# One core, local attention into two expert layers: finished rows transposed through a bank of their own and last in the step; the second batch's scale in later steps

## Chip, cores, metric

The kernel runs on one core of one Trainium2 chip, as one launch. The metric is the device time of the execution in microseconds (us). The median of three executions of the kernel before is given with the lowest and the highest; the trace is of one profiled execution.

## What is computed

The reference is an attention with a local window and 32 global tokens, followed by a gated layer and a routed layer with eight experts. For each of 4 batches and 8 heads (512 local and 32 global tokens, 64 wide):

```
s_ll = scale * q_l @ k_l.T, masked to |i - j| <= 32
s_l  = concat(scale * q_l @ k_g.T, s_ll)
out_l = softmax(s_l) @ concat(v_g, v_l)
out_g = softmax(scale * q_g @ concat(k_g, k_l).T) @ concat(v_g, v_l)
x = rows of concat(out_g, out_l)                  # 2304 tokens, 512 wide
x = (silu(x @ w_gate) * (x @ w_val)) @ w_out      # 1536 inner columns
# then routing by x @ w_gate2 to 8 experts of 288 tokens each, relu(x @ w1) @ w2
```

## The kernel before, in words

All of it is one program on one core; TensorE, VectorE, ACT and GpSimd work side by side, SP issues the transfers. The local attention is cut into 32 units (batch, half of the sequence, pair of heads), each with two windows of 128 queries. Units 0 to 15 (batches 0 and 1) are done by `front()` before anything else; the other 16 and the global tokens are worked in between the blocks of the first expert layer later. Four units with the same half make two tiles of 128 finished rows of 512, 256 tokens together; `x0_t` transposes a tile, so that it can be the moving operand of the gated layer, and splits it into a high half in fp16 (`xth`, by ACT) and a low half (`xtl`, the difference, by VectorE). The first three 256-token blocks are worked through together by `first_blocks()` (`gates` makes the two inner products, `out` the product with `w_out`), the rest by `moe_block()`; then come routing and the eight experts.

`front()` is a pipeline by hand, one window a step, steps 0 to 37. In step s it works on four windows:
- window s: its scores, four matmuls into bank S or X1 (`t` is the unit's tile);
- window s - 1: VectorE takes mask and maximum (`sm`, two rows), ACT the exponential (`pb`);
- window s - 2: TensorE transposes `pb` into a bank PTa or PTb (`pt_()` gives them in turn), ACT makes the high half `pth`, VectorE the low half `ptl`;
- window s - 3: `st_c` multiplies with the values, twelve small matmuls into bank PV; in odd steps `st_d` divides the unit by its sums (three rows of VectorE: `rs`, its reciprocal, `x`).

In between, in the order written, stand: one call in step s of the generator `V1 = v_all(1, True)`; `v_mul` and `v_cut` (GpSimd scales and splits a unit's values, ACT makes their high half `vh`); a call of `x0_t` if a finished tile is waiting in `later` (two come from `st_d` in each of steps 11, 19, 27 and 35, one is taken there and one in the step after); a piece of `conv()`, by `step_conv`, which turns the 64-bit weights into fp16 and fp32 pieces (mostly one row of VectorE, at times one of ACT); and, at the end, `ptl`.

`v_all(1, True)` finds the scale of batch 1's values in seven calls: load of half 0 into the buffer `gkr`, its sums of magnitudes on ACT (`v_sums`, two rows of ACT with their accumulator reads), load of half 1 into the same buffer, its sums, then three calls of `v_scale`: a maximum over the partitions with `bound` (a transpose of one column, a maximum on VectorE, a product with ones, in two pt_() tiles), and the power of two on VectorE. `v_mul` of unit 8 needs it in step 17.

From step 4 on, `ve`, `sc`, `te` and `gp` are wrapped by `InOrder` (line 50), which makes each instruction of the front follow the one before it on its engine; the trace therefore puts all of them down to L50. Instructions of other functions, `first_blocks()` above all, are not tied and are put in between by the compiler's own schedule. SP isn't wrapped.

PSUM has eight banks here: S, PV, PTa, PTb, X0, X1, and two of G. `front()` uses S, X1, PV, PTa and PTb. `XTAGS` gives the output banks of the first three blocks: X0 and X1, S and PV, PTa and PTb.

Of the kernel before, what the change touches and what calls it, by code (L numbers as in the profile page):

```python
# [33 lines left out]
def body(ctx, tc, units, gk, gv, wts, w2g, w1, w2, cst, cst2, out):  # L34
# [40 lines left out]
    def mark(ins):  # L75

        TURN[:] = [ins]
# [10 lines left out]
    def psb(tag):  # L88

        return ps.tile([128, 512], F32, name=tag, tag=tag, bufs=2 if tag == "G" else 1)  # L90

    def pt_():

        pts[0] ^= 1
        return psb("PT" + "ab"[pts[0]]).rearrange("p (c q) -> p c q", c=4)
# [10 lines left out]
    def load_unit(u):  # L106

        while UQ and UQ[0] <= u + (4 if UQ[0] < 4 * NA else 2):
            v = UQ.pop(0)
            if v < 4 * NA and v % 8 < len(PLACES):  # L110
                t = PLACES[v % 8]
            else:
                t = ld.tile([128, UW], F32, name="unit", bufs=UB)
            sy.dma_start(t, units[v])
            UT[v] = t
# [3 lines left out]
    def gk_tile():  # L119
        return ld.tile([128, 1280], F32, name="gkr", bufs=1)  # L120
# [58 lines left out]

    def bound(src):  # L180

        pt = pt_()
        te.transpose(pt[:1, 0, :], src, ident)
        m = wk.tile([1, 1], F32, name="pm", bufs=2)
        ve.tensor_reduce(m, pt[:1, 0, :], axis=AX.X, op=OP.max)
        yield
        pt = pt_()
        te.matmul(pt[:, 0, :1], one[:1], m, start=True, stop=True)
        yield pt[:, 0, :1]

# [79 lines left out]
    def v_sums(b, g):  # L270

        if g == 0:
            VM[b] = wk.tile([128, 4], F32, name="vm2", bufs=2)
        r = GVT.pop((b, g)).rearrange("p c w -> p (c w)")
        for i in range(2):
            sc.activation(junk, r[:, 640 * i:640 * i + 640], AF.Abs, accum_out=VM[b][:, 2 * g + i:2 * g + i + 1])

    def v_scale(b):
        m = wk.tile([128, 1], F32, name="vm", bufs=2)
        ve.tensor_reduce(m, VM.pop(b), axis=AX.X, op=OP.add)  # L280
        ve.tensor_scalar(m, m, 2.0 ** -96, None, op0=OP.max)
        iv = big.tile([128, 1], F32, name=f"iv{b}")
        parts = bound(m)
        next(parts)
        yield
        p = next(parts)
        yield
        VS[b] = pow2(p, 1, iv)
        IVB[b] = iv

    def v_all(b, own):

        for g in range(2):
            load_gv(b, g, own)
            yield
            v_sums(b, g)
            yield
        if own:
            yield from v_scale(b)
            yield  # L300
# [11 lines left out]
    X0 = {}  # L312
# [76 lines left out]
    def st_c(u, w):  # L389
        ph, pl = PTH.pop((u, w))  # L390
        vh, vl = UV[u]
        if w == 0:
            PVB[u] = psb("PV")[:, :260].rearrange("p (w h d) -> p w h d", w=2, h=2)
        pv = PVB[u]
        for h in range(2):
            n = 0
            for c in range(2):
                for a, v, m in ((ph, vh, 65), (ph, vl, 64), (pl, vh, 65)):
                    te.matmul(pv[:, w, h, :m], a[:112, 2 * h + c, :], v[:, 4 * w + 2 * c + h],  # L399
                              start=(n == 0), stop=(n == 5))  # L400
                    n += 1
        if w == 1 and u >= 4 * NA:
            st_d(u)

    def st_d(u):
        pv = PVB[u]
        hp = u % 4
        r = wk.tile([128, 2, 2], F32, name="rs")
        ve.tensor_scalar(r, pv[:, :, :, 64], P15 * 1e-9, None, op0=OP.add)
        ve.reciprocal(r, r)  # L410
        if hp == 0:
            X0[u // 4] = wk.tile([128, 2, DM], F32, name="x0", bufs=1)
        x0 = X0[u // 4]
        ve.tensor_tensor(x0[:, :, 128 * hp:128 * hp + 128].rearrange("p w (h d) -> p w h d", h=2),
                         pv[:, :, :, :64],
                         r[:, :, :, None].to_broadcast([128, 2, 2, 64]), op=OP.mult)
        del PVB[u], UT[u], UV[u]
        KQ.pop(u, None)

    def x0_t(k, src, t, n):  # L420
        if t == 0:
            if k == 2:
                XT[k] = [ld.tile([128, 5, 256], F16, name=n, bufs=1)[:, :4] for n in ("vch", "vcl")]
            elif k == 3:
                p = gk_tile().bitcast(F16)
                XT[k] = [p[:, o:o + 1024].rearrange("p (d t) -> p d t", d=4) for o in (0, 1024)]
            else:
                XT[k] = [wk.tile([128, 4, 256], F16, name=n) for n in ("xth", "xtl")]
        h, l = XT[k]
        pt = pt_()  # L430
        for d in range(4):
            te.transpose(pt[:, d, :], src[:, 128 * d:128 * d + 128], ident)
        s = slice(128 * t, 128 * t + 128)
        sc.activation(h[:, :, s], pt, AF.Copy)  # L434
        ve.tensor_tensor(l[:, :, s], pt, h[:, :, s], op=OP.subtract)  # L435
# [197 lines left out]
    def front():  # L633


        n = 8 * NA
        SS = {}
        nonlocal ve, sc, te, gp
        engines = ve, sc, te, gp
        later = []  # L640
        V1 = v_all(1, True)
        for s in range(n + 6):
            if s == 4:
                ve, sc, te, gp = map(InOrder, engines)
            at = lambda d: divmod(s - d, 2)
            if 2 <= s < n + 2:
                u, w = at(2)
                pt = pt_()
                pb = PB.pop((u, w))
                for h in range(2):  # L650
                    for c in range(2):
                        te.transpose(pt[:112, 2 * h + c, :], pb[:, h, 112 * c:112 * c + 112], ident)
                ph = wk.tile([128, 4, 128], F16, name="pth")
                pl = wk.tile([128, 4, 128], F16, name="ptl")
                sc.activation(ph[:112], pt[:112], AF.Copy, scale=P15)
            if 4 <= s and s % 2 and s - 5 < n:
                u = (s - 5) // 2
                if u >= 0:
                    st_d(u)
                    if u % 4 == 3:  # L660
                        x0 = X0.pop(u // 4)
                        later.extend((u // 4, x0[:, t], t, 256) for t in range(2))
            if 1 <= s < n + 1:
                u, w = at(1)
                S = SS.pop((u, w))
                sm = wk.tile([128, 2, WIN], F32, name="sm", tag="sm")
                mx = wk.tile([128, 2], F32, name="mx")
                for h in range(2):
                    mark(ve.tensor_tensor_reduce(sm[:, h], S[:, h, :WIN], mask[:, 2 * ((u // 4) % 2) + w], -0.125, BIG,
                                                 OP.add, OP.min, mx[:, h:h + 1]))  # L670
                pb = wk.tile([128, 2, WIN], F32, name="pb")
                for h in range(2):
                    sc.activation(pb[:, h], sm[:, h], AF.Exp, bias=mx[:, h:h + 1], scale=-1.0)
                PB[u, w] = pb
            if s < n:
                u, w = at(0)
                t = UT[u]
                S = psb("X1" if w else "S").rearrange("p (h c) -> p h c", h=2)
                for h in range(2):
                    o = UK + 256 * h + 128 * w  # L680
                    te.matmul(S[:, h, :WIN], t[:, o:o + 128], t[:, 128 * w:128 * w + WIN], start=True, stop=True)
                SS[u, w] = S
                if w == 0:
                    load_unit(u)
            if 3 <= s < n + 3:
                st_c(*at(3))
            if s < 2:
                v_sums(0, s)
            if s == 2:
                for _ in v_scale(0):  # L690
                    pass
                v_mul(0)
                v_cut(0)
            if 4 <= s < 12:
                next(V1, None)
            if s % 2 and 3 <= s < n:
                v_mul(s // 2)
            if s % 2 == 0 and 4 <= s <= n:
                v_cut(s // 2 - 1)
            if later and s - 2 < n + 4:  # L700
                x0_t(*later.pop(0))
            if s >= 5:
                step_conv()
            if 2 <= s < n + 2:
                u, w = at(2)
                mark(ve.scalar_tensor_tensor(pl[:112], pt[:112], P15, ph[:112], op0=OP.mult, op1=OP.subtract))
                PTH[u, w] = ph, pl
        while later:
            x0_t(*later.pop(0))
        ve, sc, te, gp = engines  # L710

    def v_mul(u):
        r = UT[u][:112, UK + 512:]
# [611 lines left out]
```

## Time and profile before

| | us |
|---|---|
| median of 3 executions | 960.69 (960.13 to 963.97) |
| profiled execution, its own time | 965.33 |
| its span, first to last instruction | 963.6 |
| TensorE busy | 871.9 (90% of the span) |
| VectorE busy | 611.1 (63%) |
| ACT busy | 453.0 (47%) |
| GpSimd busy | 371.9 (39%) |

The span is what the trace covers; the 1.7 us to the execution's own time lie around it. Starts in the trace are counted from the span's start. PE is TensorE's matmuls, PEld its weight loads, DVE VectorE, POOL GpSimd, SP the transfers' queue. The granted clock is a share of 2.4 GHz. A bracket at a timeline's row gives how long the engine had stood idle before it, and what released it. Names stand for tiles without their buffer numbers; digits at the end of a name are left out.

### The profile page before, as it was taken

Reading aid. Unit: us, or ns where it says so; the run is one execution under the profiler, and the core shown is the slowest. Engines: PE = TensorE matmul, PEld = TensorE weight load, DVE = VectorE, ACT = ScalarE, POOL = GpSimd, SP = SyncE. Lnnn points to the kernel's source line nnn. Section 1 sums busy time; section 2 is a strip of 40 time slices with the busy share of each in tenths; the row PEclk is TensorE's granted clock in tenths of the full one; section 3 lists DMA queues with packets and bytes.
Section 4 is the critical chain, followed back from the end, with each engine's and each line's share of the span. In section 5 each row is a group of like instructions: output and inputs, shape, how many; then the busy total and the mean of one; then the engine's idle time right before and its main releaser. Section 6 shows DMA issues by size and latency. Waiting matters only on the chain.

```text
span 963.6 us, 19509 instructions
## 1 busy us (share of the span) xinstructions
PE 871.9 (90%) x7556; PEld 732.3 (76%) x7556; DVE 611.1 (63%) x1859; ACT 453.0 (47%) x923; POOL 371.9 (39%) x344
## 2 busy tenths in 40 slices
PE   5677699999999999989979989996789989999996
PEld 4566578777788887778758757783488988999996
DVE  3677699999328579597595484268666766763210
ACT  4656454555247465445354333230554364545531
POOL 2444333444212222113111111121666786687841
PEclk8889889999999999989989999997789999999998
DMA  9631243542212233303221020001454455446600
GB/s 373 254 121 45 86 155 132 160 161 66 88 66 93 85 103 108 118 29 109 82 78 56 27 74 1 1 23 43 169 184 142 133 185 188 135 149 215 197 28 26
DMA packets 28497, 108.10 MB, mean 112 GB/s; under 512 B 3572, under 2 KB 3572, under 8 KB 28276
## 3 DMA queue, kind: packets, MB, share of 16 engines
q1 hardware_dynamic: 25332, 97.94, 30.0%
q0 software_dynamic: 3072, 8.92, 2.6%
q8 instruction: 59, 0.97, 0.4%
q14 instruction: 34, 0.28, 0.1%
HBM read 97.92 MB, written 8.91 MB: 111 GB/s over the span
## 4 chain that ended last, share of the span: by engine, by line
PE 68%; DVE 12%; issue 7%; DMA 5%; POOL 4%; ACT 3%; SPq 0%; POOLq 0%; ACTq 0%; DVEq 0%
PE G L564 26%; PE X L588 11%; PE A L1152 7%; PE A L1136 5%; PE rt L961 2%; DMA er<-w 2%; DMA xg<-xs,idx 2%; DVE junk L523 2%; DVE ge L948 1%; POOL wp L50 1%; PE PV L476 1%; PE PV L399 1%; POOL vl L50 1%; PE T L1101 1%; DMA gkr<-gv 1%
## 5 line engine op out<-in xcount | busy, mean ns | idle before, releaser
L564 PEld LDWEIGHTS <-wp 128*128 128x128 f16 x2592 | 231.6, 99 | 80.5 <-issue 52.0
L564 PE MATMUL G<-xth,wp 128*128 128x256 f16 (+1 forms) x1344 | 235.8, 270 | 4.1 <-ACT xth L434 2.5
L578 POOL TENSOR_TENSOR hl<-th,hh 128x256 fp32r<-128x256 f32 (+1 forms) x108 | 85.5, 792 | 348.1 <-ACT hh L576 274.8
L564 PE MATMUL G<-xtl,wp 128*128 128x256 f16 (+1 forms) x672 | 177.5, 270 | 4.3 <-DVE xtl L435 4.3
L1083 POOL TENSOR_TENSOR el<-er,eh 128x1024 fp32r<-128x1024 f32 x62 | 146.3, 2390 | 40.7 <-ACT eh L1080 40.4
L569 ACT ACTIVATE th<-G,ib 128x256 f32<-128x256 f32 (+1 forms) x108 | 49.4, 459 | 107.8 <-PE G L564 97.0
L571 DVE SCALAR_TENSOR_TENSOR th<-th,G 128x256 f32<-128x256 f32 (+1 forms) x108 | 43.4, 402 | 81.9 <-ACT th L569 81.0
L1080 ACT ACTIVATE eh<-er 128x1024 fp32r<-128x1024 f32 x64 | 65.5, 1054 | 49.4 <-DMA er<-w 43.2
L576 ACT ACTIVATE hh<-th 128x256 fp32r<-128x256 f32 (+1 forms) x108 | 43.4, 402 | 75.4 <-DVE th L573 75.1
L1136 PE MATMUL A<-xh,eh 128*128 128x272 f32 x256 | 77.9, 304 | 0.0
L1152 PE MATMUL A<-fh,eh 128*128 128x272 f32 x256 | 76.6, 302 | 0.0
L1136 PE MATMUL A<-xh,el 128*128 128x272 f32 x256 | 75.2, 294 | 0.0
L1136 PE MATMUL A<-xl,eh 128*128 128x272 f32 x256 | 74.9, 293 | 0.0
L1152 PE MATMUL A<-fh,el 128*128 128x272 f32 x256 | 74.4, 292 | 0.0
L1152 PE MATMUL A<-fl,eh 128*128 128x272 f32 x256 | 74.2, 291 | 0.0
L1141 DVE SCALAR_TENSOR_TENSOR fl<-A,fh 128x272 fp32r<-128x272 f32 x64 | 28.0, 439 | 59.2 <-ACT fh L1140 57.4
L523 DVE SCALAR_TENSOR_TENSOR junk<-xr,w2gt 128x512 f16<-128x512 f32 x80 | 59.0, 737 | 4.1 <-ACT xr L500 3.4
L588 PE MATMUL X<-oh,hh 128*128 128x512 f32 x156 | 57.7, 444 | 2.1 <-ACT hh L576 2.1
L588 PE MATMUL X<-oh,hl 128*128 128x512 f32 x156 | 55.7, 428 | 0.0
L573 DVE SCALAR_TENSOR_TENSOR th<-th,ib,G 128x256 f32<-128x256 f32 (+1 forms) x108 | 50.1, 464 | 2.9
L588 PE MATMUL X<-ol,hh 128*128 128x512 f32 x156 | 51.5, 403 | 0.0
L1136 PEld LDWEIGHTS A<-xl,eh 128*128 128x128 f32 x256 | 49.2, 192 | 0.1
(389 smaller groups left out, 2126.7 us busy)
## 6 DMA issues: line engine op xcount, KB each, us to landing
er<-w SPq DMA_DIRECT2D x64, 512.0 KB, 5.2
wr<-wts SPq DMA_DIRECT2D x36, 512.0 KB, 3.6
unit<-units SPq DMA_DIRECT2D x22, 688.0 KB, 4.0
unit<-gv SPq DMA_DIRECT2D x12, 640.0 KB, 3.8
wp<-units SPq DMA_DIRECT2D x10, 688.0 KB, 7.8
gkr<-gk SPq DMA_DIRECT2D x8, 608.0 KB, 4.7
xs<-xr SPq DMA_DIRECT2D x17, 256.0 KB, 2.0
gkr<-gv SPq DMA_DIRECT2D x4, 640.0 KB, 7.3
```

Of the source, the lines that this page charges most:

```text
L523: ve.scalar_tensor_tensor(junk[:, :DM], xr, 1.0, w2gt[:, e], op0=OP.mult, op1=OP.mult, accum_out=L[:, c, e:e + 1])
L564: te.matmul(pg[:, j, :n], wp_[:, f, j, a, o], x[:, d, :n], start=(i == 0), stop=(i == 11))
L569: TH[:] = [sc.activation(th[:, :n], pg[:, 0, :n], AF.Tanh, scale=ib[:, 0, f:f + 1])]
L571: ve.scalar_tensor_tensor(t[:, :n], th[:, :n], 1.0, pg[:, 0, :n], op0=OP.add, op1=OP.mult)
L573: mark(ve.scalar_tensor_tensor(h[:, :n], t[:, :n], ib[:, 1, f:f + 1], pg[:, 1, :n], op0=OP.mult, op1=OP.mult))
L576: sc.activation(hh[:, :n], h[:, :n], AF.Copy)
L578: gp.tensor_tensor(hl[:, :n], h[:, :n], hh[:, :n], op=OP.subtract)
L588: te.matmul(self.px[t], a[:, 128 * t:128 * t + 128], w[:, f, :], start=(f == 0 and i == 0), stop=(f == NF - 1 and i == 2))
L1080: q = sc.activation(h, r, AF.Copy)
L1083: q = (ve if j == 0 and i < 2 else gp).tensor_tensor(l, r, h, op=OP.subtract)
L1136: behind(te.matmul(pa_[:, :CAP], a[:, s], x[:, d], start=(i == 0), stop=(i == 11)))
L1152: behind(te.matmul(py[:, :CAP], a[:, s], x[:, f], start=(i == 0), stop=(i == 23)))
```

## The change

A function `spare()` gives a tile in bank X0 as long as `front()` runs and one by `pt_()` afterwards (`FRONT` is emptied at its end). `bound` and `x0_t` take their banks from it. V1 is called in steps 4, 8, 9, 12, 13, 14 and 15 instead of each step from 4 to 11: the load of half 0 stays in step 4, its sums go from 5 to 8, the load of half 1 from 6 to 9, its sums from 7 to 12, and the three calls of `v_scale` from 8, 9 and 10 to 13, 14 and 15. The call of `x0_t` goes to the end of the step, behind `step_conv` and `ptl`; the condition that is dropped there held in every step.

```
--- before.py
+++ after.py
@@ -88,6 +88,12 @@
     def psb(tag):
 
         return ps.tile([128, 512], F32, name=tag, tag=tag, bufs=2 if tag == "G" else 1)
+
+    FRONT = [True]
+
+    def spare():
+
+        return psb("X0").rearrange("p (c q) -> p c q", c=4) if FRONT else pt_()
 
     def pt_():
 
@@ -179,12 +185,12 @@
 
     def bound(src):
 
-        pt = pt_()
+        pt = spare()
         te.transpose(pt[:1, 0, :], src, ident)
         m = wk.tile([1, 1], F32, name="pm", bufs=2)
         ve.tensor_reduce(m, pt[:1, 0, :], axis=AX.X, op=OP.max)
         yield
-        pt = pt_()
+        pt = spare()
         te.matmul(pt[:, 0, :1], one[:1], m, start=True, stop=True)
         yield pt[:, 0, :1]
 
@@ -427,7 +433,7 @@
             else:
                 XT[k] = [wk.tile([128, 4, 256], F16, name=n) for n in ("xth", "xtl")]
         h, l = XT[k]
-        pt = pt_()
+        pt = spare()
         for d in range(4):
             te.transpose(pt[:, d, :], src[:, 128 * d:128 * d + 128], ident)
         s = slice(128 * t, 128 * t + 128)
@@ -691,23 +697,24 @@
                     pass
                 v_mul(0)
                 v_cut(0)
-            if 4 <= s < 12:
+            if s in (4, 8, 9, 12, 13, 14, 15):
                 next(V1, None)
             if s % 2 and 3 <= s < n:
                 v_mul(s // 2)
             if s % 2 == 0 and 4 <= s <= n:
                 v_cut(s // 2 - 1)
-            if later and s - 2 < n + 4:
-                x0_t(*later.pop(0))
             if s >= 5:
                 step_conv()
             if 2 <= s < n + 2:
                 u, w = at(2)
                 mark(ve.scalar_tensor_tensor(pl[:112], pt[:112], P15, ph[:112], op0=OP.mult, op1=OP.subtract))
                 PTH[u, w] = ph, pl
+            if later:
+                x0_t(*later.pop(0))
         while later:
             x0_t(*later.pop(0))
         ve, sc, te, gp = engines
+        FRONT.clear()
 
     def v_mul(u):
         r = UT[u][:112, UK + 512:]
```

## Rows read from the trace of the kernel before

**Rows 1.** Stretches: us; PE, PEld, DVE, ACT, POOL busy (instructions); granted clock; DMA share; GB/s

```profile
20.00:128.00 108.00, 78.27 (x706) 65.61 (x705) 76.05 (x247) 63.58 (x139) 45.43 (x40) 0.84 0.41 142
128.00:212.80 84.80, 84.80 (x639) 68.11 (x638) 78.22 (x150) 45.80 (x102) 33.53 (x48) 1.00 0.45 150
...
32.50:35.00 2.50, 0.00 (x0) 0.00 (x0) 0.00 (x0) 1.08 (x3) 0.00 (x0) 1.00 0.93 371
37.50:42.50 5.00, 4.63 (x27) 4.20 (x28) 4.44 (x18) 2.01 (x5) 3.10 (x2) 0.50 0.41 123
```

**Rows 2.** Who DVE waited for in 20 to 128 us

```profile
DVE xtl L50 <- ACT xth L50: 10.5, 4, 4.0
...
DVE vcl L50 <- ACT vch L50: 5.6, 2, 3.7
DVE vm L50 <- ACT junk L50: 4.5, 1, 4.5
```

**Rows 3.** Timeline of DVE; start us, us, engine line op, [idle before <-releaser]

```profile
29.85 0.68 DVE L50 SCALAR_TENSOR_TENSOR ptl<-PTa,pth 112x512 f16<-112x512 f32 x1
...
35.61 0.16 DVE L50 TENSOR_REDUCE vm<-vm 128x1 f32<-128x4 f32 x1 [4.47 <-ACT junk L50]
...
43.37 0.69 DVE L50 SCALAR_TENSOR_TENSOR ptl<-PTb,pth 112x512 f16<-112x512 f32 x1 [0.65 <-ACT pth L50]
...
57.53 0.68 DVE L50 SCALAR_TENSOR_TENSOR ptl<-PTa,pth 112x512 f16<-112x512 f32 x1
...
67.81 0.37 DVE L50 CUSTOM_DVE_ANT_0 sm<-X,mask 128x224 f32<-128x224 f32 x1
...
68.43 0.69 DVE L50 SCALAR_TENSOR_TENSOR wp<-wr,wp 128x512 int32<-128x512 int32 x1
69.04 0.69 DVE L50 SCALAR_TENSOR_TENSOR ptl<-PTb,pth 112x512 f16<-112x512 f32 x1
69.64 0.15 DVE L50 TENSOR_SCALAR rs<-PV 128x4 f32<-128x4 f32 x1
...
70.38 0.38 DVE L50 CUSTOM_DVE_ANT_0 sm<-S,mask 128x224 f32<-128x224 f32 x1
...
72.85 0.69 DVE L50 TENSOR_TENSOR xtl<-PTb,xth 128x512 f16<-128x512 f32 x1 [1.77 <-ACT xth L50]
...
74.06 0.68 DVE L50 SCALAR_TENSOR_TENSOR ptl<-PTa,pth 112x512 f16<-112x512 f32 x1
...
81.20 0.69 DVE L50 SCALAR_TENSOR_TENSOR ptl<-PTa,pth 112x512 f16<-112x512 f32 x1
...
94.17 0.67 DVE L50 SCALAR_TENSOR_TENSOR ptl<-PTb,pth 112x512 f16<-112x512 f32 x1
...
108.05 0.68 DVE L50 SCALAR_TENSOR_TENSOR ptl<-PTa,pth 112x512 f16<-112x512 f32 x1
...
119.99 0.68 DVE L50 SCALAR_TENSOR_TENSOR ptl<-PTa,pth 112x512 f16<-112x512 f32 x1
...
130.11 0.69 DVE L50 TENSOR_TENSOR gkr<-PTa,gkr 128x512 f16<-128x512 f32 x1 [0.48 <-ACT gkr L50]
```

**Rows 4.** Timeline of ACT

```profile
33.89 0.74 ACT L50 ACTIVATE junk<-gkr 128x640 f16<-128x640 f32 x1 [4.32 <-DMA gkr<-gv]
...
70.87 0.85 ACT L50 ACTIVATE pb<-sm,mx 128x224 f32<-128x224 f32 x2 [0.24 <-DVE mx L50]
72.22 0.60 ACT L50 ACTIVATE xth<-PTb 128x512 f16<-128x512 f32 x1 [0.51 <-PE PTb L50]
74.18 0.72 ACT L50 ACTIVATE junk<-wp,tiny 128x512 f16<-128x512 f32 x1 [1.36 <-DVE wp L50]
...
76.85 0.62 ACT L50 ACTIVATE vh<-wp 112x512 f16<-112x512 f32 x1
```

**Rows 5.** Timeline of PE

```profile
49.25 0.87 PE L50 MATMUL PTa<-ident,pb 128*112 128x128 f32 x4 [2.44 <-DVE ptl L50]
...
122.50 1.22 PE L588 MATMUL X<-oh,hh 128*128 128x512 f32 x2 [0.68 <-ACT hh L576]
```

More of the change, by code (lines that the diff above doesn't have):

```diff
@@ L90, in psb, with spare @@
         return ps.tile([128, 512], F32, name=tag, tag=tag, bufs=2 if tag == "G" else 1)
+    FRONT = [True]
+    def spare():
+        return psb("X0").rearrange("p (c q) -> p c q", c=4) if FRONT else pt_()
     def pt_():
@@ L180, in bound @@
     def bound(src):
-        pt = pt_()
+        pt = spare()
         te.transpose(pt[:1, 0, :], src, ident)
@@ L186, in bound @@
         yield
-        pt = pt_()
+        pt = spare()
         te.matmul(pt[:, 0, :1], one[:1], m, start=True, stop=True)
@@ L429, in x0_t @@
         h, l = XT[k]
-        pt = pt_()
+        pt = spare()
         for d in range(4):
@@ L693, in front @@
                 v_cut(0)
-            if 4 <= s < 12:
+            if s in (4, 8, 9, 12, 13, 14, 15):
                 next(V1, None)
@@ L699, in front @@
                 v_cut(s // 2 - 1)
-            if later and s - 2 < n + 4:
-                x0_t(*later.pop(0))
             if s >= 5:
@@ L707, in front @@
                 PTH[u, w] = ph, pl
+            if later:
+                x0_t(*later.pop(0))
         while later:
@@ L710, in front @@
         ve, sc, te, gp = engines
+        FRONT.clear()
     def v_mul(u):
```

## The prediction

> **What bounds the kernel now.** I read the page first (TensorE busy nearly throughout, least in the first slices and at a lower clock there), then the stretches, the waits of VectorE, and the timelines of the first attention. The stretches show two regimes [rows 1]. From 128 us on TensorE is busy all the time at 2.4 GHz: what ends earlier before that point ends the program earlier. From 20 to 128 us, where the change lies, TensorE is busy for 78.3 of 108 us at a mean granted clock of 0.84, and VectorE for 76.1: no engine is full, so the steps of `front()` are bound by who waits for whom.
>
> VectorE makes one `ptl` in each step from 2 to 33, so the starts of `ptl` are the clock of the steps: that of step 7 is at 29.85, of step 10 at 43.37, 13 at 57.53, 18 at 69.04, 21 at 81.20, 26 at 94.17, 29 at 108.05, 33 at 119.99 [rows 3]. Steps 14 to 18, without anything special, take (69.04 - 57.53) / 5 = 2.30 us each. Three groups of steps take far more than 3 x 2.30 = 6.9 us:
> - 8 to 10, with the second batch's sums and scale: 13.52 us;
> - 11 to 13, with the first finished rows: 14.16 us;
> - 19 to 21 and 27 to 29, with the second and third pair of row tiles: 12.16 and 13.88 us.
>
> The waits say why [rows 2]. VectorE waited 10.5 + 5.6 = 16.1 us, in six waits, for the high halves (`xth`, `vch`) of `x0_t`, and 4.5 us for the sums of batch 1. TensorE waited for VectorE in turn: the transposes of step 12 stood 2.44 us before `ptl` of step 11 had freed PTa [rows 5], since `x0_t` had taken PTb out of turn.
>
> **The change, part by part.** I take the step's order and durations from the rows and lay the new order out by hand. On VectorE, starts of rows that follow each other give what each takes: `sm` pair 0.62, conversion 0.61, `ptl` 0.60, `st_d` 0.74 (69.64 to 70.38) [rows 3]; an `xtl` row is 0.69, with 0.60 to the next start. On ACT `pb` takes 0.85, an accumulating conversion row 0.72, `vh` 0.62, `xth` 0.60 [rows 4].
>
> *V1 later, steps 8 to 10.* Now the second load for batch 1 waits for the buffer that step 5's sums free, so step 7's sums wait 4.32 us for it [rows 4], VectorE 4.47 for the sums [rows 3], and TensorE stands empty from 32.5 to 35 [rows 1]. Afterwards step 8 sums the first half, step 9 issues the second load, step 12 sums it: some three steps of cover, 7 us or more, while the transfers are at a 0.93 share only until about 35 us. The load's issue moves on SP's queue too: it waits for ACT in step 8, and what stands behind it (unit 10 for step 20, weight words for step 17) is needed some eight steps later, so I cost that at nothing; if the cover failed, ACT would wait in step 12 as it now does in step 7, 4.3 us. In step 8 the sums cost ACT 1.7 us (33.89 until VectorE's `vm` goes at 35.61). Laid out, `ptl` of step 8 goes at 31.5, step 9 at 35.3 (behind sums, `vh`, conversion, `pth` on ACT), step 10 at 37.3: 7.4 us instead of 13.52, **-6.1**. Ends: -4.5 (only VectorE's wait goes) and 6.9 - 13.52 = -6.6.
>
> *Bank and order, steps 19 to 21.* Nothing changes until `sm` of step 18 ends at 71.0. The conversion and `ptl` of step 19 then go at once, to 72.2. The finished rows' transposes are where they were, so `xth` could start at 72.22, but the conversion's ACT row now stands ahead: `xth` about 72.5, `xtl` 73.1 to 73.7. Step 20's transposes find PTb free and run at 72.2, no longer behind `ptl`. But `sm` of step 19 now stands behind `xtl`: 73.7 to 74.3, conversion and `ptl` to 74.9 at the latest; on ACT `pb` starts at 74.05, then `vh`, a conversion row, and `xth` only at 76.1; `xtl` 76.65 to 77.25; then `st_d`, `sm`, conversion: `ptl` of step 21 at 79.25 instead of 81.20, **-2.0**. Three steps then take 10.2 us. Ends: 0 (the wait only changes its place) and 6.9 + 2 x 0.60 - 12.16 = -4.1 (all of it hidden).
>
> A rule of the Trainium skill speaks against the bank: by Perfetto Trace Analysis, Optimizing Tensor Performance (Matmuls), independent groups should rotate through banks, so that emptying one overlaps filling the next, and here every spare tile sits in the one bank X0. By it the second tile would wait for the first's `xtl`. In the layout that costs nothing: X0 is free at 73.7 and the second tile's transposes come up at 73.9, behind `st_c`.
>
> *Steps 27 to 29.* The same 10.2 us against 13.88, **-3.7**; ends 0 and -5.8.
>
> *Steps 11 to 13.* The same 10.2, and now with the sums of step 12 on ACT (1.7) and the scale's way VectorE, TensorE, VectorE in step 13 (some 0.9): 12.8 against 14.16, **-1.4**; ends 0 and -3.3. The scale's end in steps 14 and 15 adds **+0.5**, ends 0 and 1.
>
> *The hand-over.* The fourth pair of tiles (steps 35, 36) isn't needed until block 3, so its place costs nothing by itself. But it now uses X0, and X0 is the first bank into which the first blocks write, at 122.50 [rows 5]; the last `x0_t` has its bank read at 130.11 + 0.69 = 130.80 [rows 3]. TensorE's queue is in order: if the first output waited for it, it would lose up to 8.3 us; nothing, if VectorE ends the tiles first. I take **+2.2**: what is pushed into the full stretch is the six outputs of one block, 3.7 us at the 1.22 us per two of this row, somewhat over half of it at the full clock.
>
> Sum: -6.1 - 2.0 - 3.7 - 1.4 + 0.5 + 2.2 = -10.5 us. The profiled execution took 965.33 us (span 963.6), 4.64 over the median shown, 960.69; the forecast is 954.8 for such an execution, so **950.2** for the median. All ends together: 20 us gained to 5 lost.
>
> **The rivals.**
> - *TensorE gets warmer (0.15).* After the empty stretch the granted clock is 0.50 from 37.5 to 42.5 [rows 1], that is 1.2 GHz. The mean of 0.84 over 108 us says that about a third of them, 35 us, ran at that level. If half of that went and a quarter of its time were on the path, some 4.5 us more are gained: 945.7. The Trainium skill's TensorE: Matmul & The Clock Gate, HAM oscillation, says the same of idle waits between bursts: they bring the half clock back; the empty 2.5 us with 0.50 after them agree. For it: the waits named go. Against: the ones left may still suffice.
> - *The hand-over costs all of its 8.3 us (0.12).* Then -12.7 + 8.3 = -4.4: 956.3, no change to speak of. For it: TensorE's queue is in order, and VectorE gets to the last tile 10 us after the last `ptl` [rows 3]. Against: the output matmuls may be queued behind other work.
> - *The wait only moves, from bank to ACT (0.05 even, 0.08 worse).* `xth` is last on ACT, `xtl` last on VectorE, and the next `sm`, then `pb`, stand behind it. If the three pairs gain nothing, -6.1 + 0.5 + 2.2 = -3.4: 957.3. If each of the six steps loses an ACT `pb` and `vh` on top, about 1.5 us, that is 9 us: 966.3, slower. It decides from 3.4 / 6 = 0.57 us per step: VectorE's mean wait before `xtl` would have to rise from 16.1 / 6 = 2.7 to over 3.3 us. Against: the order by hand gives it 0.4 and 1.7.
> That the change doesn't do what it says is unlikely: on VectorE, ACT, TensorE and GpSimd `front()` runs in written order from step 4.
>
> **How the numbers follow.** The forecast has 0.60, the rivals the rest. A measurement can tell about 0.5%, 4.8 us. Faster by more: 0.60 + 0.15 = 0.75; within: 0.12 + 0.05 = 0.17; slower: 0.08. The range goes from 944 (the warm rival and half of what the upper ends add to it) to 958 (past the two cases without change).
>
> **What would show it.** Right: `ptl` of step 10 near 37 us, no ACT wait on the `gkr` load, `ptl` of 19 and 20 no longer behind `xtl`; `ptl` of step 33 near 107; from there the same tail with the full stretch at 117 or 118. Wrong: a wait of over 2 us before `xtl` in most of the six steps; an X output matmul that waits for the last `xtl`; or a full stretch that starts earlier and yet ends as late.

## The result, and the profile after

The changed kernel takes 949.41 us (median of 4 executions, 943.45 to 952.47) against 961.79 (960.13 to 963.97) for the kernel before in the same comparison: ratio 0.9861, 95% interval 0.9821 to 0.9901, 1.4% faster. Its profiled execution took 952.47 us, span 950.7, against 965.33 and 963.6: 12.9 us less. TensorE's busy time is the same, 871.8 us to 871.9. Lines moved by six: L564, L576 and L588 of the kernel before are L570, L582 and L594 here.

The stretches of the changed kernel, with the columns of [rows 1]:

```profile
20.00:118.00 98.00, 79.48 (x723) 65.27 (x723) 78.18 (x253) 66.03 (x145) 49.28 (x45) 0.84 0.48 166
118.00:201.40 83.40, 83.40 (x624) 66.79 (x623) 76.55 (x144) 43.69 (x97) 32.41 (x44) 1.00 0.45 142
32.50:35.00 2.50, 2.21 (x22) 1.56 (x21) 2.43 (x10) 2.47 (x6) 0.50 (x1) 1.00 0.90 359
37.50:42.50 5.00, 5.00 (x44) 4.53 (x43) 3.61 (x13) 3.90 (x9) 3.52 (x3) 0.66 0.92 302
```

The full stretch starts 10 us earlier. Ahead of it TensorE does the same work (79.5 us, before 78.3) in 98 us where it took 108, so its idle time there fell from 29.7 to 18.5 us. The stretch that was empty is full (2.21 of 2.50 us). The granted clock of the stretch from 37.5 to 42.5 us rose from 0.50 to 0.66, but its mean over the front is 0.84, as before.

The waits of VectorE in 20 to 118 us (us in total, times, longest) answer to [rows 2]:

```profile
DVE xtl L50 <- ACT xth L50: 5.3, 4, 2.0
...
DVE vcl L50 <- ACT vch L50: 1.5, 2, 1.0
```

16.1 us before the low halves became 6.8, and the 4.5 us for the sums of batch 1 are gone from the list. VectorE's timeline, to be read beside [rows 3]:

```profile
31.49 0.68 DVE L50 SCALAR_TENSOR_TENSOR ptl<-PTa,pth 112x512 f16<-112x512 f32 x1
...
38.66 0.69 DVE L50 SCALAR_TENSOR_TENSOR ptl<-PTb,pth 112x512 f16<-112x512 f32 x1 [0.49 <-ACT pth L50]
...
48.00 0.69 DVE L50 TENSOR_TENSOR xtl<-X,xth 128x512 f16<-128x512 f32 x1 [2.05 <-ACT xth L50]
...
51.56 0.67 DVE L50 SCALAR_TENSOR_TENSOR ptl<-PTa,pth 112x512 f16<-112x512 f32 x1
...
65.82 0.68 DVE L50 SCALAR_TENSOR_TENSOR ptl<-PTa,pth 112x512 f16<-112x512 f32 x1
67.27 0.69 DVE L50 TENSOR_TENSOR xtl<-X,xth 128x512 f16<-128x512 f32 x1 [0.76 <-ACT xth L50]
...
70.86 0.69 DVE L50 TENSOR_TENSOR xtl<-X,xth 128x512 f16<-128x512 f32 x1 [1.68 <-ACT xth L50]
...
73.49 0.68 DVE L50 SCALAR_TENSOR_TENSOR ptl<-PTa,pth 112x512 f16<-112x512 f32 x1
...
107.03 0.68 DVE L50 SCALAR_TENSOR_TENSOR ptl<-PTa,pth 112x512 f16<-112x512 f32 x1
...
119.62 0.69 DVE L50 TENSOR_TENSOR gkr<-X,gkr 128x512 f16<-128x512 f32 x1 [0.82 <-ACT gkr L50]
```

These are `ptl` of steps 7 (31.49), 10, 13 (51.56), 19 (65.82), 21 (73.49) and 33. `ptl` of step 19 stands 1.45 us ahead of the low half of its finished rows; before, it stood behind it (`xtl` 72.85, `ptl` 74.06 [rows 3]). ACT, beside [rows 4]:

```profile
33.54 0.72 ACT L50 ACTIVATE junk<-gkr 128x640 f16<-128x640 f32 x1
...
45.29 0.72 ACT L50 ACTIVATE junk<-gkr 128x640 f16<-128x640 f32 x1
...
46.87 0.61 ACT L50 ACTIVATE vh<-unit 112x512 f16<-112x512 f32 x1
47.39 0.58 ACT L50 ACTIVATE xth<-X 128x512 f16<-128x512 f32 x1
```

The first sums (33.54) and the second (45.29) wait for no load any more; but the second sums, step 12, stand ahead of `vh` and `xth`, and VectorE waits 2.05 us at 48.00. With the scale's calls as before (e2 and e4 below) the same wait is 0.47 us.

The groups of steps, as differences of the starts of `ptl`, in us, with the granted clock of the stretch in brackets, here and for the experiments below:

| kernel | 8-10 | 11-13 | 14-18 | 19-21 | 22-26 | 27-29 | 30-33 | step 4 to 33 | step 33 to the end |
|---|---|---|---|---|---|---|---|---|---|
| before | 13.52 (0.75) | 14.16 (0.84) | 11.51 (0.90) | 12.16 (0.96) | 12.97 (0.91) | 13.88 (0.86) | 11.94 (0.88) | 98.03 | 843.6 |
| changed | 7.17 (0.94) | 12.90 (0.90) | 11.66 (0.71) | 10.27 (1.00) | 11.44 (1.00) | 9.92 (1.00) | 12.18 (0.82) | 83.52 | 843.7 |
| e1 | 7.13 (0.95) | 18.02 (0.69) | 12.52 (0.80) | 13.53 (0.87) | 11.67 (1.00) | 14.52 (0.67) | 13.17 (0.85) | 98.55 | 839.9 |
| e2 | 12.81 (0.75) | 9.66 (0.98) | 10.81 (0.84) | 10.27 (1.00) | 13.12 (0.87) | 9.92 (1.00) | 10.88 (1.00) | 85.41 | 838.7 |
| e3 | 12.19 (0.72) | 11.79 (1.00) | 10.88 (0.84) | 11.44 (1.00) | 11.45 (1.00) | 11.80 (0.95) | 10.74 (0.89) | 88.03 | 838.8 |
| e4 | 13.11 (0.74) | 9.66 (1.00) | 10.17 (1.00) | 10.27 (1.00) | 11.45 (1.00) | 9.92 (1.00) | 10.92 (1.00) | 83.37 | 843.1 |
| e5 | 7.72 (0.87) | 12.33 (0.92) | 10.26 (0.87) | 10.26 (1.00) | 11.45 (1.00) | 9.92 (1.00) | 11.32 (1.00) | 80.72 | 842.7 |
| e6 | 7.48 (0.90) | 12.60 (0.91) | 13.03 (0.76) | 10.26 (1.00) | 13.12 (0.87) | 9.92 (1.00) | 10.93 (1.00) | 85.04 | 844.5 |
| e7 | 7.50 (1.00) | 8.76 (1.00) | 12.10 (0.86) | 10.26 (1.00) | 11.46 (1.00) | 9.92 (1.00) | 12.05 (0.86) | 79.92 | 841.7 |
| e8 | 7.49 (0.90) | 10.01 (0.91) | 12.00 (1.00) | 10.27 (1.00) | 13.13 (0.87) | 9.91 (1.00) | 10.93 (1.00) | 81.43 | 841.7 |
| e9 | 7.55 (0.89) | 12.52 (0.91) | 10.26 (0.86) | 10.27 (1.00) | 11.45 (1.00) | 9.92 (1.00) | 11.33 (1.00) | 80.92 | 866.4 |
| e10 | 7.50 (1.00) | 8.76 (1.00) | 11.25 (1.00) | 10.26 (1.00) | 11.45 (1.00) | 9.91 (1.00) | 10.93 (1.00) | 77.93 | 845.7 |
| e11 | 7.50 (1.00) | 8.76 (1.00) | 11.45 (0.85) | 10.26 (1.00) | 11.45 (1.00) | 9.91 (1.00) | 10.92 (1.00) | 78.35 | 838.2 |
| e12 | 7.51 (1.00) | 8.76 (1.00) | 11.44 (0.85) | 10.27 (0.98) | 12.86 (0.88) | 9.92 (1.00) | 12.10 (0.86) | 80.96 | 840.2 |

At the hand-over TensorE shows the collision in bank X0 (beside [rows 5]):

```profile
110.13 0.80 PE L594 MATMUL X<-oh,hh 128*128 128x512 f32 x1 [0.94 <-ACT hh L582]
...
115.61 0.44 PE L570 MATMUL G<-vch,wp 128*128 128x256 f16 x1
...
120.37 0.50 PE L594 MATMUL X<-oh,hh 128*128 128x512 f32 x1
```

Before, the first output wrote two X tiles at once (x2, 122.50); now one is written at 110.13 and the other, X0's, only at 120.37, after the last `x0_t` has had that bank read (119.62 + 0.69). In between TensorE goes on with the gates (115.61). Yet from `ptl` of step 33 to the end both kernels take the same time, 843.6 and 843.7 us.

### The profile page after: what moved, and what is told of

Same layout as the page of the kernel before. It is cut to its first block, busy times and chain, and to the rows that moved or that the text cites. A ratio compares the mean times of both kernels' runs of the same rounds, so it can differ in the third digit from the quotient of the medians.

```text
span 950.7 us, 19506 instructions
## 1 busy us (share of the span) xinstructions
PE 871.8 (92%) x7556; PEld 727.9 (77%) x7556; DVE 612.0 (64%) x1859; ACT 451.7 (48%) x923; POOL 372.8 (39%) x344
## 4 chain that ended last, share of the span: by engine, by line
PE 68%; DVE 11%; issue 7%; DMA 6%; POOL 4%; ACT 4%; SPq 0%; POOLq 0%; ACTq 0%
PE G L570 26%; PE X L594 11%; PE A L1159 7%; PE A L1143 6%; DMA xg<-xs,idx 3%; DMA er<-w 2%; DVE junk L529 2%; PE rt L968 2%; PE PV L482 1%; PE PV L405 1%; DVE ge L955 1%; POOL el L1090 1%; PE S L449 1%; DMA gkr<-gv 1%; PE T L1108 1%
## 5 line engine op out<-in xcount | busy, mean ns | idle before, releaser
L570 PEld LDWEIGHTS <-wp 128*128 128x128 f16 x2592 | 231.8, 99 | 79.2 <-issue 51.4
L570 PE MATMUL G<-xth,wp 128*128 128x256 f16 (+1 forms) x1344 | 235.7, 270 | 2.7 <-ACT xth L440 2.3
L570 PE MATMUL G<-xtl,wp 128*128 128x256 f16 (+1 forms) x672 | 177.4, 270 | 3.9 <-DVE xtl L441 3.4
L575 ACT ACTIVATE th<-G,ib 128x256 f32<-128x256 f32 (+1 forms) x108 | 49.4, 459 | 108.7 <-PE G L570 97.9
L577 DVE SCALAR_TENSOR_TENSOR th<-th,G 128x256 f32<-128x256 f32 (+1 forms) x108 | 43.4, 402 | 79.7 <-ACT th L575 78.7
L582 ACT ACTIVATE hh<-th 128x256 fp32r<-128x256 f32 (+1 forms) x108 | 43.3, 401 | 72.6 <-DVE th L579 72.3
L594 PE MATMUL X<-oh,hh 128*128 128x512 f32 x156 | 57.9, 443 | 2.4 <-ACT hh L582 2.4
L594 PE MATMUL X<-oh,hl 128*128 128x512 f32 x156 | 56.2, 428 | 0.0
L579 DVE SCALAR_TENSOR_TENSOR th<-th,ib,G 128x256 f32<-128x256 f32 (+1 forms) x108 | 50.2, 464 | 2.8
L594 PE MATMUL X<-ol,hh 128*128 128x512 f32 x156 | 51.3, 401 | 0.0
```

The lines of the kernel that those rows point to most:

```text
L570: te.matmul(pg[:, j, :n], wp_[:, f, j, a, o], x[:, d, :n], start=(i == 0), stop=(i == 11))
L575: TH[:] = [sc.activation(th[:, :n], pg[:, 0, :n], AF.Tanh, scale=ib[:, 0, f:f + 1])]
L577: ve.scalar_tensor_tensor(t[:, :n], th[:, :n], 1.0, pg[:, 0, :n], op0=OP.add, op1=OP.mult)
L579: mark(ve.scalar_tensor_tensor(h[:, :n], t[:, :n], ib[:, 1, f:f + 1], pg[:, 1, :n], op0=OP.mult, op1=OP.mult))
L582: sc.activation(hh[:, :n], h[:, :n], AF.Copy)
L594: te.matmul(self.px[t], a[:, 128 * t:128 * t + 128], w[:, f, :], start=(f == 0 and i == 0), stop=(f == NF - 1 and i == 2))
```

## The experiments

Diffs are against the changed kernel; `bound`, where nothing else is said, is put back into the pt_() tiles. All kernels compute the whole reference.

**e1: the scale's calls alone.** `x0_t` goes back to its place ahead of `step_conv` and to PTa and PTb.

```
-        pt = spare()
+        pt = pt_()
...
+            if later:
+                x0_t(*later.pop(0))
             if s >= 5:
                 step_conv()
...
-            if later:
-                x0_t(*later.pop(0))
```

> Only the later calls of V1; bank and place of x0_t as before. Theory (the parts add up): steps 8 to 10 take 7.2 us instead of 13.5, steps 11 to 13 get the sums and the scale on top of the old waits, about 16.7 instead of 14.2, the pairs stay at 12.2 and 13.9; 3 to 4 us faster than before, ratio 0.996. Rival (the clock): once the empty stretch at 33 us is gone TensorE stays at 2.4 GHz in the following steps and the gain is over 8 us, ratio 0.991 or less.

Measured: 962.99 us, ratio 1.0011 (0.9986 to 1.0036). Both missed. Steps 8 to 10 gained 6.4 us, as by the prediction; steps 11 to 13 lost 3.9, 14 to 18 one more, and 19 to 33 another 1.9, where the granted clocks differ too. VectorE's row of step 12 in the kernel before, then two rows of VectorE and two of ACT in this one:

```profile
53.76 0.69 DVE L50 TENSOR_TENSOR xtl<-PTb,xth 128x512 f16<-128x512 f32 x1 [4.05 <-ACT xth L50]
```

```profile
49.57 0.69 DVE L50 TENSOR_TENSOR xtl<-PTb,xth 128x512 f16<-128x512 f32 x1 [4.65 <-ACT xth L50]
...
55.08 0.28 DVE L50 TENSOR_REDUCE pm<-PTb 1x1 f32<-1x128 f32 x1 [2.01 <-PE PTb L50]
```

```profile
46.86 0.72 ACT L50 ACTIVATE junk<-gkr 128x640 f16<-128x640 f32 x1
...
48.96 0.57 ACT L50 ACTIVATE xth<-PTb 128x512 f16<-128x512 f32 x1
```

The sums that left step 7 stand in step 12 between VectorE and its `xth`, and with `xtl` still ahead of `ptl` the whole step waits with it. But that wait was 4.05 us already, so it accounts for only 0.6 of the 3.9 us. In step 13 VectorE waits 2.01 us more for the transpose of the scale (`pm`), and the small rows of the scale are added.

**e2: bank and place, the scale's calls as before.**

```
-            if s in (4, 8, 9, 12, 13, 14, 15):
+            if 4 <= s < 12:
```

> x0_t last in the step and in bank X0; V1 in steps 4 to 11 and its scale in PTa and PTb as before. Theory: steps 8 to 10 stay at 13.5 us, 11 to 13 come down to about 10.3, 19 to 21 to 10.3, 27 to 29 to 9.9; 10 to 11 us faster, ratio 0.989. Rival (the wait only moves from the bank to ACT): under 2 us, ratio 0.998 or more.

Measured: 948.75 us, ratio 0.9863 (0.9818 to 0.9908), the whole of the change's gain. The theory held, with a somewhat larger gain than it gave. Steps 11 to 13 take 9.66 us, against 12.90 with the scale's calls moved.

**e3: the bank alone** (e2, and `x0_t` back ahead of `step_conv`, in X0).

> x0_t in bank X0, but ahead of the conversion and of ptl as before; V1 as before. Theory (the place in the step gives most): VectorE still waits for xth ahead of ptl, only the transposes of the next step come earlier; about 1 us per pair, 3 us in all, ratio 0.997. Rival (the bank gives most): 8 us or more, ratio 0.992 or less.

Measured: 951.87 us, ratio 0.9911 (0.9881 to 0.9940). The rival held: a bank of its own brings about two thirds of the gain (0.0089 of 0.0137) even where `x0_t` is ahead of `ptl`.

**e4: the place alone** (e2, and `x0_t` in PTa and PTb).

```
         h, l = XT[k]
-        pt = spare()
+        pt = pt_()
```

> x0_t last in the step, but in PTa and PTb by turns; V1 as before. Theory (the place gives most): ptl now goes ahead of xtl, so the bank that x0_t took out of turn is free when the next step asks for it; 9 us or more, ratio 0.991, within 1 us of the kernel with bank and place. Rival (the bank gives most): the transposes go on waiting, 3 us or less, ratio 0.997 or more.

Measured: 947.44 us, ratio 0.9854 (0.9815 to 0.9894). The theory held: the place alone brings all of it. VectorE's timeline of e4 at the second pair, beside 67.27 and 70.86 of the changed kernel:

```profile
67.19 0.69 DVE L50 TENSOR_TENSOR xtl<-PTb,xth 128x512 f16<-128x512 f32 x1 [0.76 <-ACT xth L50]
...
70.78 0.69 DVE L50 TENSOR_TENSOR xtl<-PTb,xth 128x512 f16<-128x512 f32 x1 [1.68 <-ACT xth L50]
```

The waits are the same to the hundredth with the bank and without, and so are the groups (10.27 and 9.92). TensorE's waits before the transposes into PTa, in the kernel before (20 to 128 us) and then in e4 (20 to 116 us):

```profile
PE PTa L50 <- DVE ptl L50: 7.8, 3, 2.7
PE PTa L50 <- DVE rs L50: 5.8, 3, 2.7
```

```profile
PE PTa L50 <- DVE ptl L50: 2.5, 4, 1.1
```

In e4 the waits on `rs` are gone and those on `ptl` fell from 7.8 to 2.5 us; in e2 and e3 neither is listed. So bank and place are two ways to the same thing: the next step's transposes wait little or not at all for a bank that the finished rows hold. In e3, where `xtl` still stands ahead of `ptl`, TensorE waits in PV instead, 6.5 us for `x` and 5.1 for `ptl`. The Trainium skill, Perfetto Trace Analysis, Optimizing Tensor Performance (Matmuls), wants independent groups to rotate through banks. The pair of banks (e4, 0.9854) and the single one (e2, 0.9863) differ here by less than the intervals, so these runs show no price for the single bank.

**e5: the changed kernel once more,** on another chip, beside e6 to e8; nothing is edited.

> The changed kernel once more, beside the next three on one chip. Both theories: ratio 0.986 to before within 0.004, ptl from step 4 to 33 in 83.5 us within 1.5 us; where a five-step group without finished rows differs from its fellow in another run by over 1 us, the granted clock in it differs too.

Measured: 949.77 us, ratio 0.9839 (0.9804 to 0.9874). The ratio held; the length from step 4 to 33, 80.72 us, missed its bound by 1.3 us. It differs from the first profile most in steps 14 to 18, where the clock does, as the expectation had it: 10.26 us at 0.87 here, 11.66 at 0.71 there. The stretch of steps 14 to 18 in the changed kernel, then in e5 (columns of [rows 1]):

```profile
51.56:63.22 11.66, 11.16 (x98) 9.76 (x97) 10.14 (x43) 7.96 (x18) 6.62 (x8) 0.71 0.47 145
```

```profile
50.25:60.51 10.26, 9.76 (x100) 8.42 (x98) 10.05 (x43) 7.90 (x18) 6.62 (x8) 0.87 0.51 166
```

The first busy time is TensorE's, the third VectorE's: VectorE's is nearly the same, TensorE's differs by 1.4 us, and so does the group.

**e6: the scale's calls moved, the place late, nothing in X0** (the changed kernel with pt_() for spare() throughout).

> x0_t last in the step and the later calls of V1, but nothing in bank X0: tiles and scale in PTa and PTb by turns. Theory (place and bank remove the same wait, the place alone is enough): ptl from step 4 to 33 within 1.5 us of the changed kernel's 83.5, ratio 0.986. Rival (with sums and scale among the finished rows the bank is needed): steps 11 to 15 longer by 3 us or more, ratio 0.990 or more.

Measured: 953.19 us, ratio 0.9857 (0.9826 to 0.9889). The theory held in the ratio and at the very edge of its length (85.04 us). Against e4 it gains 5.6 us in steps 8 to 10 and loses 2.9 in 11 to 13 and 2.9 in 14 to 18, the latter at a clock of 0.76 against 1.00: nothing is left. With the bank that is not so clear. From e2 to the changed kernel 5.6 us are gained, 3.2 and 0.9 lost; from e2 to e5, the same changed kernel, 5.1 are gained, 2.7 lost in 11 to 13, and 14 to 18 are 0.6 shorter.

**e7: the second sums in step 9,** the first back in step 5 and the second load back in step 6.

```
-            if s in (4, 8, 9, 12, 13, 14, 15):
+            if s in (4, 5, 6, 9, 10, 13, 14):
```

> The changed kernel with V1 called in steps 4, 5, 6, 9, 10, 13 and 14: the second half's sums in step 9, the transpose of the scale in step 10, so that neither stands in the steps with finished rows. Theory (the later V1 gives back in steps 11 to 15 what it gains in 8 to 10, because ACT has no room beside xth): 8 to 10 in about 8.5 us instead of 7.2, 11 to 13 in 9.8 instead of 12.9, 14 to 18 in 10.8 instead of 11.7; 2.5 to 3 us less from step 4 to 33, ratio about 0.983. Rival (the load is what counts): step 9 waits for the load as step 7 did, 2 us or more, and the ratio stays at 0.986 or more.

Measured: 946.42 us, ratio 0.9783 (0.9753 to 0.9813), below the 0.983 that was expected and the 0.9839 of the changed kernel beside it (e5), where the two intervals just overlap. The rival missed: in step 9 ACT doesn't wait for the load. Steps 8 to 10 keep their gain (7.50), 11 to 13 take 8.76 us, and 14 to 18, at a clock of 0.86, 12.10 where 10.8 was expected. ACT in e7:

```profile
35.11 0.72 ACT L50 ACTIVATE junk<-gkr 128x640 f16<-128x640 f32 x1
...
43.92 0.57 ACT L50 ACTIVATE xth<-X 128x512 f16<-128x512 f32 x1
```

The second sums run at 35.11, a step without finished rows, and their load is there; in step 12 no sums stand between `pb` and `xth`, only `vh`, and VectorE's wait for it is 0.46 us instead of 2.05. The scale's first transpose has left step 13 as well; no run moves the sums without it.

**e8: the second sums in step 13,** the three calls of `v_scale` in 14 to 16.

> The changed kernel with V1 called in steps 4, 8, 9, 13, 14, 15 and 16: the second half's sums one step later, out of the second step with finished rows, the scale behind them. Theory (ACT has no room beside xth): 11 to 13 in about 11 us instead of 12.9, 14 to 18 about 1 us longer, 1 us less in all. Rival (the scale's way between VectorE and TensorE is what costs): 11 to 18 together as before, 24.6 us within 0.4.

Measured: 948.98 us, ratio 0.9815 (0.9787 to 0.9843). Steps 11 to 13 take 10.01 us, 14 to 18 12.00 at full clock, against 10.17 in e4. The rival missed (22.0 us for steps 11 to 18, not 24.6). The theory held for the groups; that it makes the kernel faster isn't shown, since the interval overlaps that of e5. Out of the way of the finished rows, the sums (1.7 us) and the scale's way (some 1.0) together cost 1.8 us in steps 14 to 18.

**e9: the fourth pair alone back in PTa and PTb,** to free X0 for the hand-over. `k` is the number of the pair.

```
-        pt = spare()
+        pt = spare() if k != 3 else pt_()
```

> The changed kernel, with only the fourth pair of finished tiles (steps 35 and 36) back in PTa and PTb, so that bank X0 is free when the first blocks write it. Theory (the collision in X0 is real, but what it pushes back is made up in the full stretch): the first output of the first blocks writes two X tiles again, as in the kernel before, and the length from ptl of step 33 to the end of the span stays at 843.7 us within 3 us; the time is within 0.3% of the changed kernel's, ratio to the kernel before 0.983 to 0.989. Rival (my prediction's term: the hand-over costs 2.2 us or more): the length falls by 2 us or more below the lowest of the changed program's (842.7), to under 841, and the ratio by 0.003.

Measured: 972.19 us, ratio 1.0072 (1.0046 to 1.0099): both missed, and the kernel is slower than the one before. The front is as fast as in the changed kernel (`ptl` of step 33 at 104.01); from there to the end it takes 866.4 us, 22.7 more. Stretch and TensorE's waits of e9:

```profile
130.00:250.00 120.00, 99.88 (x709) 79.39 (x707) 87.62 (x169) 50.99 (x114) 38.00 (x54) 0.99 0.29 103
```

```profile
PE G L570 <- DVE th L579: 18.9, 17, 1.4
```

In the stretch that is otherwise full TensorE stands idle for 20 us and waits 17 times for `th`, VectorE's last row of a gate (the waits are those of 118 to 250 us). ACT's timeline and then VectorE's show why:

```profile
159.80 0.74 ACT L282 ACTIVATE junk<-unit 128x640 f16<-128x640 f32 x1
...
162.03 0.84 ACT L575 ACTIVATE th<-G,ib 128x256 f32<-128x256 f32 x2 [0.55 <-PE G L570]
```

```profile
162.54 0.79 DVE L577 SCALAR_TENSOR_TENSOR th<-th,G 128x256 f32<-128x256 f32 x2 [3.28 <-ACT th L575]
163.24 0.47 DVE L579 SCALAR_TENSOR_TENSOR th<-th,ib,G 128x256 f32<-128x256 f32 x1
```

On ACT the tanh (L575) of two gates run as a pair, behind conversions and sums (the row at 159.80 is one of them) and only once the second gate's products are there, so the earlier gate's comes late; on VectorE their two first rows (L577) follow as a pair, and only then the earlier gate's last row (L579), which frees its bank G for TensorE. The first blocks aren't tied by `InOrder`; the order of VectorE's two rows (F for L577, L for L579) begins so in the traces:

```
before, changed, e4, e7:  FFLLFLFLFLFLFLFLFLFLFLFLFLFLFLFLFLFLFLFL
e9:                       FFLLFLFLFLFFLLFLFFLLFLFFLLFLFFLLFLFFLLFL
```

**e10: e7 with the finished tiles in PTa and PTb,** only `bound` in X0.

> The calls of V1 in steps 4, 5, 6, 9, 10, 13 and 14, as in the best kernel so far (ratio 0.978), but the finished tiles in PTa and PTb again, still last in the step; only the scale's two small tiles lie in X0. Theory (with the late place the own bank adds nothing): steps 19 to 21 and 27 to 29 take 10.3 and 9.9 us again, steps 8 to 13 together 16.3 us within 1; ratio 0.976 to 0.983. Rival (the bank is needed for the gain of the earlier sums): steps 11 to 13 take over 10.5 us, ratio 0.985 or more.

Measured: 949.06 us, ratio 0.9834 (0.9804 to 0.9864): at the theory's edge, a hair outside. The front is as it said (8 to 13 in 16.3 us, 10.26 and 9.91 for the pairs, `ptl` of step 33 at 101.14); the rest, 845.7 us, is 7.5 longer than in e11. Up to 400 us the two traces keep together (787 and 783 matmuls between 300 and 400 us); they part behind it, where the edited choice of a bank is no longer in force. Why they part stays open.

**e11: e7 once more,** beside e9 and e10 on one chip.

> The best kernel so far once more, beside the two others on one chip: V1 in steps 4, 5, 6, 9, 10, 13 and 14, finished tiles in X0 and last. Theory (sums in step 9 keep what the later scale gains, since no finished rows stand in that step): steps 8 to 13 take 16.3 us within 1 and the ratio is 0.975 to 0.982, below the changed kernel's 0.984 to 0.986. Rival (the 0.978 was a lucky draw of the clock): 0.984 or more.

Measured: 943.28 us, ratio 0.9784 (0.9758 to 0.9811). The theory held, with steps 8 to 13 in 16.3 us again. It is 5.8 us faster than e10, which lacks only the finished tiles' own bank; between e2 and e4 the bank made no such difference.

**e12: e9 with the scale's calls of e7.** Its rows alternate, like those of the changed kernel.

> The kernel before this one that was slower (fourth pair of finished tiles in PTa and PTb, the other three in X0), now with V1 in steps 4, 5, 6, 9, 10, 13 and 14. In the slower one VectorE's compiled order of the first blocks has, in every round, one block's first row of the gate (th<-th,G) ahead of the last row of the block before; in this one the two alternate from the third round on, as in the changed kernel. Theory (that order made the slower one slow, not the bank of the fourth pair): from ptl of step 33 to the end of the span 838 to 846 us, TensorE waits less than 3 us in all for th between 118 and 250 us, ratio to the kernel before 0.975 to 0.983. Rival (the fourth pair in PTa and PTb, with the others in X0, is what costs): the length is over 855 us and TensorE waits over 10 us for th, ratio 0.995 or more.

Measured: 947.06 us, ratio 0.9796 (0.9769 to 0.9822). The theory held: 840.2 us from step 33 to the end, and TensorE between 118 and 250 us:

```profile
PE G L570 <- DVE th L579: 0.2, 1, 0.2
```

So the 22.7 us of e9 are not the price of the fourth pair's bank; they come with the order of the first blocks' rows. e12 is also the test of the hand-over that e9 was meant to be, since only the fourth pair's bank parts it from e7 and e11. Its first output writes both X tiles at once again:

```profile
107.51 1.22 PE L594 MATMUL X<-oh,hh 128*128 128x512 f32 x2 [1.53 <-ACT hh L582]
```

In e7 and e11 X0's output comes 10 us behind X1's, as in the changed kernel; yet the rest takes 841.7 and 838.2 us there and 840.2 here.

## Why the prediction was right, and where its steps were not

The forecast, 950.2 us, stands 0.8 from the median; that is partly luck. In the comparison the kernel before stood at 961.79 and not 960.69, so 12.4 us were gained where 10.5 were forecast; between the profiled executions it is 12.9. By its steps:

- *Steps 8 to 10, -6.1:* measured -6.35; `ptl` of step 10 at 38.66, no ACT wait on the load. Right. With what steps 11 to 15 were to pay for it (2.6 + 0.5 us) the working leaves the scale's move a net gain of 3.0 us. Alone it brought nothing (e1, 1.0011). With the late place, steps 8 to 18 take 33.3 and 32.9 us with the calls as before (e2, e4) and 31.7, 30.3, 33.1 and 30.3 with the changed calls (changed, e5, e6, e9): from 3.0 us shorter to 0.2 longer, and the clock in 14 to 18 differs among them. The ratios (0.9863 and 0.9854; 0.9861, 0.9839 and 0.9857) can't tell 3 us, 0.3%, either. So whether that gain is there stays open.
- *Steps 11 to 13, -1.4:* measured -1.26, in part by luck: without the scale's move they take 9.66 us (e2, e4) for the 10.2 laid out, and the move adds 3.2 us to e2, or 2.7 to 2.9 in e5, e6 and e9, for 2.6. The working had the mechanism. In the changed kernel VectorE waits 2.86 us for `xth` in this group, in e2 1.11; the scale's way takes about 1.0 us (49.97 to 50.97), as the 0.9 of the prediction; the rest of the 3.2 us is a wait for PV that is 0.45 us longer. Its ends were not well set: with the sums added the upper end is -3.5 by its own terms, not -3.3, and the lower end, 0, leaves out that sums and scale come on top where the old waits stay (e1: +3.9).
- *Steps 19 to 21, -2.0, and 27 to 29, -3.7:* measured -1.89 and -3.96. In the eleven profiles with `x0_t` last, these groups repeat within 0.02 us, so this part, laid out by hand, was right in size and place; the waits before `xtl`, 0.76 and 1.68, were given as 0.4 and 1.7. The layout leans on the bank ("Step 20's transposes find PTb free"); the place alone does as well (e4).
- *Steps 14 and 15, +0.5:* 14 to 18 measured +0.15, but at a clock of 0.71 against 0.90, and -1.25 in e5 at 0.87. The clock hides the term; no run shows it by itself.
- *The hand-over, +2.2:* measured +0.1. The collision is in the trace as described (X0's output comes 10 us after X1's), but other gates fill the time. The seven profiles with all finished tiles in X0 (changed, e2, e3, e5, e7, e8, e11) take 838.2 to 843.7 us from step 33 to the end, the five with all of them in PTa and PTb (before, e1, e4, e6, e10) 839.9 to 845.7: no loss. e12 without the collision stands between e7 and e11 with it. This is the term that was mis-sized: it should have been 0, its lower end, and the rival of 8.3 us falls with it. e9 says nothing on it, since the order of the blocks changed with it. The premise that TensorE is busy all the time from 128 us on goes too far (8.59 of 10 us between 220 and 230 us before, at a clock of 0.85), but the rest kept its length.
- *Not foreseen:* -1.5 us in steps 22 to 26, and +1.6 up to `ptl` of step 7. The first goes with the clock (0.91 to 1.00); the same steps take 13.12 us at 0.87 in e2 and e6 (last section). Of the second, the start of step 4 lies between 21.9 and 23.5 us among kernels with the same text up to there, so I count it as scatter.

Of the rivals, that the wait only moves is half true, for one of the parts: the load's wait went, and the wait for `xth` behind the sums stayed at 2.05 us; for the six steps together it fell, 16.1 to 6.8 us. A warmer TensorE isn't needed for the gain: the mean clock of the front stayed at 0.84. In e4 it is 1.00 from step 11 to 33, without a clearly better time (0.9854 against 0.9861). The Trainium skill, TensorE: Matmul & The Clock Gate, HAM oscillation, has idle waits between bursts bring back the half clock; the stretch from 37.5 to 42.5 us, 0.50 behind the empty one and 0.66 without it, agrees in part. Steps 14 to 18 are at 0.71 in one profile and 0.87 in another of the same kernel, so a clock of one profile is no term of a sum.

## What to carry to other kernels

In a pipeline written out by hand, first move the stalling work behind the work that the next step waits for; a bank of its own brought two thirds of that by itself (e3) and nothing on top that e2 and e4 could show. When an instruction is moved to be covered, look at what stands behind it on its own engine in the new step: 1.7 us of sums and 1.0 of the scale's way cost 2.7 to 3.2 where the finished rows queue behind them, and next to nothing three steps earlier (ratio 0.978 to 0.983 in place of 0.984 to 0.986). Where part of the order is the compiler's, compare the order of the rows in both kernels before reading a difference as the price of an edit.

## What the runs showed that was not expected

- An edit of one bank choice, at a place that costs nothing by itself (e12), made the kernel 22.7 us longer behind it (e9), with the rows of two gates as pairs on ACT and VectorE, in 7 places where the other kernels alternate. What makes the compiler choose that order stays open.
- The length behind the front scatters by 7.5 us among profiles with the same alternating order there (838.2 to 845.7 us); what sets it wasn't tried. So a difference below some 0.8% between these variants is not settled by one trace of each.
- Steps 22 to 26, without finished rows, take 11.45 us at full clock and 13.12 at 0.87, with the same instructions: in the front the clock is worth 1.7 us in five steps, nearly what the change gained in steps 19 to 21 (1.89). The whole difference stands in one wait of VectorE for TensorE's PV, in step 23 of e2 (0.87) and then of e5 (1.00):

```profile
78.72 0.16 DVE L50 TENSOR_SCALAR rs<-PV 128x4 f32<-128x4 f32 x1 [2.12 <-PE PV L50]
```

```profile
73.79 0.16 DVE L50 TENSOR_SCALAR rs<-PV 128x4 f32<-128x4 f32 x1 [0.45 <-PE PV L50]
```

In the 3 us before `ptl` of step 21 TensorE was busy for 1.33 us at full clock in both; behind it the clock fell in e2 and not in e5. Why it fell in one of them stays open.
